# Up weights in six pieces of 512 columns, pair 1's x between the first two, and a new order of work up to pair 4's scores

## The chip, the cores and the metric

One core of one Trainium2 chip runs the whole program. The metric is device time in microseconds (us) of one execution. The engines are TensorE (PE; its weight loads are listed apart as PEld), VectorE (DVE), ScalarE (ACT), GpSimd (POOL) and the sync engine (SP), which only issues transfers. Every engine works through its own list of instructions in order and waits where an operand is not there yet.

## The reference

A chunked state-space recurrence over 4 batches, 8 heads and 768 tokens (x 32 wide, B and C 16 wide) gives y. The 256 values of a token over its heads are the input row of a bilinear feed-forward layer of 1536 hidden columns:

```
L = exp(cum_i - cum_j), causal;  M = (C B^T) * L
y = M x + (C state) * exp(cum);  state = decay * state + B^T (x * decay_from_j)
X = y, as (3072 tokens, 256)
out = ((X @ w_a) * (X @ w_b)) @ w_out        # w_a, w_b: 256 x 1536, w_out: 1536 x 256
```

## The kernel before, in words

The sequence is cut into 6 blocks of 128 tokens. A block has two pairs of batches; pair p is block p // 2, batches 2(p % 2) and the next one. There are 12 pairs. The first four pairs (two blocks, P0 = 4) are done one way, with each of their steps at a place written out by hand; the rest go by loops over blocks.

A pair goes through these steps. Its B, C and x are loaded (`load1`, L140; tiles bn, cn, xn). B and C are scaled by decay factors into bm and cm (`scale_bc`, L291, on POOL or DVE), x into f16 (`scale_x`, L282). PE transposes bm and cm (L326, needs both), ACT and DVE copy them out to bt and ct. `scores` (L353, matmuls at L373 or L358) multiplies them into four PSUM banks; each bank is masked causally into tile t by DVE, or, for the fourth one, by ACT (a copy, L410) and POOL (L411). `pv` (L467) multiplies masked scores with the scaled x (L433), adds the carried state (L477), forms the block's own state sums (`ds_mm`, L460) and evacuates the result into X2T. `state_sums` (L557) and `state_spread` (L569) turn the sums into the next block's carried state, tile sbd, on DVE and POOL.

The feed-forward part of pairs 0 to 3 is cut into units (p, k2), k2 from 0 to 5: a unit is 256 hidden columns, four matmuls of 256 columns against Wa into a bank "aps" and four against Wb into a bank "bps" (`unit_mm`, L596, matmuls at L601). ACT copies aps to SBUF (L615), DVE multiplies with bps into hk (`times`, L622). `out_mm` (L632, matmuls at L637) multiplies hk with Wo, 12 matmuls for each half pair. From block 2 on units have 512 columns (L667) and the output is at L694.

The weights are f32 in memory and are cast to f16 by the transfers that POOL issues. Before, w_a and w_b are loaded in two halves of 768 columns each (`load_w`, L162), w_out in two halves (`load_wo`, L169). A column index k of 128 hidden columns is not contiguous in the piece: it takes every third column of a run of 384 (L601 to L604), so that w_out's rows come as runs of three.

POOL issues these transfers from its own list, between its arithmetic: pair 1's B and C, Wa's first half, Wb's first half, pair 1's x (L211 to L216); after pair 1's B is scaled, Wa's and Wb's second halves and pair 2's B (L768 to L770); after pair 1's masked scores, pair 2's C, w_out's halves and pair 2's x (L797 to L804). SP issues pair 3's inputs and all that follow, in order; pair 3's B waits, by a hand-written dependence (L837), for Wb's last piece to land.

"Warm-up" matmuls on zeros (L220) fill PE's time before there is work. The order of all this is written by hand (`manual_schedule`), and the string BANKS says which of four PSUM banks each successive feed-forward tile takes.

Of the kernel before, what the change touches and what calls it, by code (L numbers as in the profile page):

```python
# [11 lines left out]
f16 = mybir.dt.float16  # L12
# [7 lines left out]
YS = 16.0  # L20

BANKS = (
    "0123102310231012301230123012031230123013201320130213021302130213021320312031203102132013"
    "2013203102310231023103210321032103210321032103210231023102310231023102310231023102310231"
)


# [1 line left out]
def kernel(  # L29
# [13 lines left out]
    nc = tc.nc  # L43
# [39 lines left out]
    big = ctx.enter_context(tc.tile_pool(name="big", bufs=1))  # L83
    a_sb = big.tile([BH, NBLK, Q], f32, name="a_sb")
    zero = big.tile([BH, Q], f32, name="zero")
    KC = d_ff // 2
    Wa = [big.tile([128, 2, KC], f16, name=f"Wa{t}") for t in range(2)]
    Wb = [big.tile([128, 2, KC], f16, name=f"Wb{t}") for t in range(2)]
    Wo = big.tile([128, NK, d_model], f16, name="Wo")
    X2T = big.tile([128, P0, 2, 2, Q], f16, name="X2T")  # L90
    XB = big.tile([128, NBLK - P0 // NBP, 2, 2, NBP, Q], f16, name="XB")
# [35 lines left out]
    def bank(name):  # L127
        return psf.tile([128, 512], f32, name=name, tag=f"ff{next(banks)}")
# [11 lines left out]
    def load1(eng, p, which, bt, i0=0, n=64):  # L140
        blk, bp = divmod(p, NBP)
        if p >= P0:
            return eng.dma_start(
                by_token(pair_in[p][which])[:, bt],
                (B, C, x)[which][2 * bp + bt, :, blk * Q : (blk + 1) * Q, :].rearrange("h q n -> q h n"),
            )
        src = (B, C, x)[which][2 * bp + bt, :, blk * Q + 2 * i0 : blk * Q + 2 * i0 + 2 * n, :]
        return eng.dma_start(  # L148
            pair_in[p][which][64 * bt + i0 : 64 * bt + i0 + n].rearrange("i h r n -> i h (r n)"),
            src.rearrange("h (i r) n -> i h (r n)", r=2),  # L150
        )
# [10 lines left out]
    def load_w(half):  # L162
        c = slice(half * KC, (half + 1) * KC)
        return [
            nc.gpsimd.dma_start(W[half], src.rearrange("(f p) e -> p f e", p=128)[:, :, c])
            for W, src in ((Wa, moe_w_a), (Wb, moe_w_b))
        ]

    def load_wo(half):  # L169
        nc.gpsimd.dma_start(  # L170
            Wo[:, 6 * half : 6 * half + 6].rearrange("p (g kk) e -> p g (kk e)", kk=3),
            moe_w_out.rearrange("(g p kk) e -> p g (kk e)", p=128, kk=3)[:, 2 * half : 2 * half + 2],
        )

    nc.sync.dma_start(a_sb, a.rearrange("b h (k q) -> (b h) k q", q=Q))
    for p_ in range(3):
# [218 lines left out]
    def product0(m2, e):  # L395

        return (
            st[0]["T1"][:, 4 * m2 : 4 * m2 + 4].rearrange("p (m e) r q -> p e m (r q)", e=2)[:, e],
            (SC0, SC1)[m2][:, :, e * 256 : e * 256 + 256],
        )  # L400

    def mask(out_in, by_pool=False, by_token=False):
        o_, i_ = out_in
        if by_token:
            c_ = causal_q.unsqueeze(1).broadcast_to((128, 4, Q))
        else:
            c_ = causal.rearrange("p r q -> p (r q)").unsqueeze(1).broadcast_to((128, 2, 2 * Q))
        if by_pool:
            tmp = mid.tile([128, *c_.shape[1:]], f32, name="tmp", tag="tmp")
            nc.scalar.copy(tmp, i_)  # L410
            nc.gpsimd.tensor_tensor(out=o_, in0=tmp, in1=c_, op=ALU.mult)  # L411
        else:
            nc.vector.tensor_tensor(out=o_, in0=i_, in1=c_, op=ALU.mult)  # L413
# [179 lines left out]
            )  # L593
        st.setdefault(("S", p + NBP), {})["Sbd"] = Sbd

    def unit_mm(p, k2, W):  # L596
        ps = bank("aps" if W is Wa else "bps")
        for kk in range(2):
            k = 2 * k2 + kk
            for f in range(2):  # L600
                nc.tensor.matmul(  # L601
                    ps[:, kk * 2 * Q : (kk + 1) * 2 * Q],
                    W[k // 6][:, f, k % 6 // 3 * 384 : (k % 6 // 3 + 1) * 384].rearrange("p (c kk) -> p kk c", kk=3)[
                        :, k % 3  # L604
                    ],
                    X2T[:, p, :, f],
                    start=(f == 0),
                    stop=(f == 1),
                    skip_group_check=True,
                )  # L610
        return ps

    def evac_a(a_ps, on_dve=False):
        asb = ffh.tile([128, 512], f32, name="asb", tag="asb")
# [44 lines left out]
    def bunit(blk, k):  # L659
        s = st.setdefault(("FF", blk), {})  # L660
        if "hk" not in s:
            s["hk"] = hkb.tile([128, NK, 2 * NBP * Q], f16, name="hkb", tag="hkb")
        ps = []
        for W in (Wa, Wb):
            t_ = bank("aps" if W is Wa else "bps")
            for f in range(2):
                nc.tensor.matmul(  # L667
                    t_,
                    W[k // 6][:, f, k % 6 // 3 * 384 : (k % 6 // 3 + 1) * 384].rearrange("p (c kk) -> p kk c", kk=3)[
                        :, k % 3  # L670
                    ],
                    XB[:, blk - P0 // NBP, f].rearrange("p t j q -> p (t j q)"),
                    start=(f == 0),
                    stop=(f == 1),
                    skip_group_check=True,
                )
# [46 lines left out]
    def go(*items):  # L723
        for p, k2 in items:
            unit(p, k2)()
# [81 lines left out]
    ds_mm(0, 64, SC[:2])  # L807
# [12 lines left out]
    for k2 in range(1, 3):  # L820
        times(0, k2, bps[k2], asb[k2])
# [10 lines left out]
    nc.gpsimd.memset(causal_q, 1.0)  # L832
    nc.gpsimd.affine_select(
        out=causal_q, in_=causal_q, compare_op=ALU.is_ge, fill=0.0, base=0, pattern=[[1, Q]], channel_multiplier=-1
    )
    b3 = [load1(nc.sync, 3, 0, bt) for bt in range(2)]
    tc.add_manual_dep(b3[0].ins, w1[1].ins.name, AFTER, reason="weights ahead of pair 3's inputs")  # L837
    for bt in range(2):
        load1(nc.sync, 3, 1, bt)
    loads_x(3, nc.sync)  # L840
    loads_bc(4)
# [14 lines left out]
    scale_x(2, nc.scalar)  # L856
    scale_bc(3, 0, nc.gpsimd)
    scale_bc(3, 1, nc.gpsimd)
    loads_bc(5)
# [5 lines left out]
    out_mm(0, 1, o[1], range(6, NK))  # L865
    out_store(0, 1, o[1])
    o_ps = bank("ops")
    out_mm(1, 0, o_ps, range(6))
# [187 lines left out]
```

## Time and profile before

| | |
|---|---|
| median of 3 runs | 122.99 us (122.73 to 124.71) |
| the profiled execution | 122.51 us, of which 120.8 us are the span of the profile |
| DVE busy | 85.2 us (71%) |
| ACT busy | 72.1 us (60%) |
| POOL busy | 62.3 us (52%) |
| HBM read and written | 11.13 MB and 3.15 MB |
| busy share of the 16 DMA engines | 0.9 or more in 3 to 24 us, by slices of 3 us |
| SP's wait for Wb's last piece before pair 3's inputs | 13.2 us, until 18.41 us |

Times in the profile are counted from the start of the span. A timeline row gives the start and the length of a run of equal instructions; for PE the length includes the time until the last result is out, so rows overlap and the distance between two starts is the rate. In brackets stands how long the engine was idle before and what ended that. A transfer's row is the time that POOL or SP spent issuing it; how long it took to land is a separate answer.

### The profile page before, as it was taken

The numbers are of one execution on the slowest core, as the hardware profiler recorded it, in microseconds if no ns is written. First come the engines' busy times: TensorE is split into PE (matmuls) and PEld (weight loads), VectorE is DVE, ScalarE is ACT, GpSimd is POOL, SyncE is SP. The second block draws the span as 40 slices with busy tenths as digits, with TensorE's granted clock in tenths as the row PEclk, the third lists the DMA queues.
The fourth block names the chain that finished last, engine by engine and source line by source line (L and its number), as shares of the span: only waits on it lengthen the run. The fifth ranks groups of instructions, "written<-read, shape, count | busy, mean of one in ns | idle before, by whom it ended". The sixth has DMA issues, their size and how long they took to land.

```text
span 120.8 us, 3711 instructions
## 1 busy us (share of the span) xinstructions
PE 115.7 (96%) x1455; PEld 79.4 (66%) x1455; DVE 85.2 (71%) x162; ACT 72.1 (60%) x142; POOL 62.3 (52%) x108
## 2 busy tenths in 40 slices
PE   5889999999999999999999999999999999999990
PEld 2445889888898898644476464766464684555890
DVE  1887888882989898499984999677799445847100
ACT  0466757854965767877668637645646737566220
POOL 7999998972795676299731993138400000000200
PEclk9999999999999999999999999999999999999999
DMA  3999999986969999699998874869501012010032
GB/s 62 171 169 233 173 201 159 215 140 70 100 99 126 128 125 144 111 135 146 71 151 111 173 239 126 91 90 159 180 3 49 0 43 87 0 49 0 20 110 87
DMA packets 66641, 13.73 MB, mean 114 GB/s; under 512 B 61616, under 2 KB 66256, under 8 KB 66624
## 3 DMA queue, kind: packets, MB, share of 16 engines
q1 hardware_dynamic: 62448, 9.40, 50.7%
q0 software_dynamic: 2176, 3.74, 17.0%
q10 hardware_dynamic: 2000, 0.36, 1.6%
q8 instruction: 11, 0.18, 0.7%
q14 instruction: 6, 0.05, 0.1%
HBM read 11.13 MB, written 3.15 MB: 118 GB/s over the span
## 4 chain that ended last, share of the span: by engine, by line
PE 89%; DMA 4%; POOL 3%; issue 0%; ACT 0%; POOLq 0%
PE ops L694 18%; PE aps L667 18%; PE bps L667 17%; PE ops L637 9%; PE aps L601 9%; PE bps L601 9%; DMA Wa<-in_moe_w_a_dram 4%; PE SC L358 2%; PE SC L419 2%; POOL cn L148 1%; PE SC L373 1%; PE SC L433 1%; PE SC L508 1%; POOL bn L148 1%; POOL causal L208 1%; PE SC L460 1%
## 5 line engine op out<-in xcount | busy, mean ns | idle before, releaser
L615 ACT COPY asb<-aps 128x512 f32<-128x512 f32 x72 | 41.8, 586 | 14.1 <-PE aps L667 9.7
L679 DVE TENSOR_TENSOR hkb<-bps,asb 128x512 f16<-128x512 f32 x48 | 32.3, 687 | 12.8 <-ACT asb L615 11.6
L667 PE MATMUL aps<-XB,Wa 128*128 128x512 f16 x96 | 28.6, 379 | 0.0
L667 PE MATMUL bps<-XB,Wb 128*128 128x512 f16 x96 | 28.5, 379 | 0.0
L694 PE MATMUL ops<-Wo,hkb 128*128 128x256 f16 (+1 forms) x204 | 22.5, 267 | 0.0
L694 PEld LDWEIGHTS <-hkb 128*128 128x128 f16 x204 | 18.5, 98 | 3.1
L413 DVE TENSOR_TENSOR t<-SC,causal_q 128x512 f16<-128x512 f32 x27 | 17.1, 681 | 3.3 <-PE SC L358 3.3
L622 DVE TENSOR_TENSOR hk<-bps,asb 128x512 f16<-128x512 f32 x24 | 16.2, 685 | 2.4 <-ACT asb L615 1.2
L667 PEld LDWEIGHTS <-Wb 128*128 128x128 f16 x96 | 9.9, 103 | 10.9
L667 PEld LDWEIGHTS <-Wa 128*128 128x128 f16 x96 | 9.7, 103 | 9.1 <-issue 0.2
L708 POOL DMA_DIRECT2D out_dram<-osb x1 | 0.6, 639 | 27.3 <-ACT osb L706 27.3
L706 ACT ACTIVATE osb<-ops 128x256 f32<-128x256 f32 (+1 forms) x16 | 6.0, 376 | 14.3 <-PE ops L694 14.2
L601 PE MATMUL aps<-X2T,Wa 128*128 128x256 f16 x96 | 14.0, 273 | 0.1
L601 PE MATMUL bps<-X2T,Wb 128*128 128x256 f16 x96 | 13.8, 273 | 0.0
L637 PE MATMUL ops<-Wo,hk 128*128 128x256 f16 x96 | 11.5, 273 | 0.0
L601 PEld LDWEIGHTS <-Wa 128*128 128x128 f16 x96 | 9.5, 104 | 1.1 <-DMA Wa<-in_moe_w_a_dram 0.3
L601 PEld LDWEIGHTS <-Wb 128*128 128x128 f16 x96 | 9.8, 103 | 0.6
L411 POOL TENSOR_TENSOR t<-tmp,causal_q 128x512 f16<-128x512 f32 x5 | 5.8, 1159 | 8.0 <-ACT tmp L410 7.9
L637 PEld LDWEIGHTS <-hk 128*128 128x128 f16 x96 | 8.9, 98 | 1.4
L304 POOL TENSOR_TENSOR bm<-bn,fB 128x256 f16<-128x256 f32 x11 | 7.1, 641 | 4.8 <-DMA bn<-in_B_dram 3.6
L289 POOL TENSOR_SCALAR x<-xn 128x512 f16<-128x512 f32 x6 | 8.9, 1489 | 1.0 <-DMA xn<-in_x_dram 0.7
L296 POOL TENSOR_TENSOR planes<-cn,fC 128x256 f16<-128x256 f32 x8 | 5.0, 621 | 7.9 <-DMA cn<-in_C_dram 7.8
(95 smaller groups left out, 124.0 us busy)
## 6 DMA issues: line engine op xcount, KB each, us to landing
out_dram<-osb SPq DMA_DIRECT2D x22, 128.0 KB, 1.8
xn<-in_x_dram SPq DMA_DIRECT2D x7, 256.0 KB, 4.3
cn<-in_C_dram SPq DMA_DIRECT2D x8, 128.0 KB, 4.1
bn<-in_B_dram SPq DMA_DIRECT2D x8, 128.0 KB, 4.6
Wa<-in_moe_w_a_dram POOLq DMA_DIRECT2D x2, 384.0 KB, 5.9
Wb<-in_moe_w_b_dram POOLq DMA_DIRECT2D x2, 384.0 KB, 7.3
Wo<-in_moe_w_out_dram POOLq DMA_DIRECT2D x2, 384.0 KB, 7.2
xn<-in_x_dram POOLq DMA_DIRECT2D x4, 128.0 KB, 7.2
```

Source lines behind the costliest of these rows:

```text
L289: eng.tensor_scalar(xo, xi, XS, None, ALU.mult)
L304: eng.tensor_tensor(out=m_, in0=raw, in1=(f[:, blk, :, bp] if factor is None else factor).unsqueeze(3).broadcast_to((128, 2, H, N)), op=AL ...
L411: nc.gpsimd.tensor_tensor(out=o_, in0=tmp, in1=c_, op=ALU.mult)
L413: nc.vector.tensor_tensor(out=o_, in0=i_, in1=c_, op=ALU.mult)
L601: nc.tensor.matmul(ps[:, kk * 2 * Q : (kk + 1) * 2 * Q], W[k // 6][:, f, k % 6 // 3 * 384 : (k % 6 // 3 + 1) * 384].rearrange("p (c kk) -> ...
L615: (nc.vector.tensor_copy if on_dve else nc.scalar.copy)(asb, a_ps)
L622: nc.vector.tensor_tensor(out=s["hk"][:, 2 * k2 : 2 * k2 + 2, :].rearrange("p k q -> p (k q)"), in0=b_ps, in1=asb, op=ALU.mult)
L637: nc.tensor.matmul(o_ps[:, 0:d_model], hk[:, k, bt * Q : (bt + 1) * Q], Wo[:, k, :], start=(k == 0), stop=(k == NK - 1), skip_group_check= ...
L667: nc.tensor.matmul(t_, W[k // 6][:, f, k % 6 // 3 * 384 : (k % 6 // 3 + 1) * 384].rearrange("p (c kk) -> p kk c", kk=3)[:, k % 3], XB[:, b ...
L679: return lambda: nc.vector.tensor_tensor(out=s["hk"][:, k], in0=ps[1], in1=asb, op=ALU.mult)
L694: nc.tensor.matmul(o_ps[:, 0:w], hk[:, k, c * Q : (c + 1) * Q], Wo[:, k, cs], start=(k == 0), stop=(k == NK - 1), skip_group_check=True,)
L706: nc.scalar.activation(out=o_sb[:, 0:w], in_=o_ps[:, 0:w], func=AF.Copy, scale=1.0 / (YS * YS))
```

## The change

Wa and Wb become three tiles each of 512 columns, so six pieces. Index k takes every fourth column of a piece (`w_cols`), and w_out's rows come as runs of four, loaded as two thirds and one third. POOL's list becomes: Wa piece 0, pair 1's x, Wb piece 0; then Wa and Wb piece 1; after pair 1's masked scores Wa and Wb piece 2, pair 2's B and C, w_out's two loads; after pair 2's B and C are scaled, pair 2's x and the tile maskbd. The clearing of `planes` and `causal_q` moves behind pair 3's scaling. SP's pair 3 waits for Wb piece 2. On PE two units (0, 0) and (0, 1) instead of three stand ahead of pair 1's `pv`, the second of them split around pair 1's scores; the order of the later units of pairs 0 to 3 changes, one warm-up matmul of 128 columns goes, and the units (2, 4) and (3, 0) come earlier. On DVE the last two scans move ahead. BANKS is another string. From pair 4's scores on the order is as before, but for the unit (3, 0), which has been done.

```diff
-    KC = d_ff // 2
-    Wa = [big.tile([128, 2, KC], f16, name=f"Wa{t}") for t in range(2)]
-    Wb = [big.tile([128, 2, KC], f16, name=f"Wb{t}") for t in range(2)]
+    KG = 4
+    KC = KG * 128
+    Wa = [big.tile([128, 2, KC], f16, name=f"Wa{t}") for t in range(NK // KG)]
+    Wb = [big.tile([128, 2, KC], f16, name=f"Wb{t}") for t in range(NK // KG)]
...
+    def load_w(W, g, f0=0, f1=2):
+        src = (moe_w_a if W is Wa else moe_w_b).rearrange("(f p) e -> p f e", p=128)
+        return nc.gpsimd.dma_start(W[g][:, f0:f1], src[:, f0:f1, g * KC : (g + 1) * KC])
...
+    def w_cols(W, k, f):
+        return W[k // KG][:, f].rearrange("p (c kk) -> p kk c", kk=KG)[:, k % KG]
...
-    load_w(0)
+    load_w(Wa, 0)
     for bt in range(2):
         load1(nc.gpsimd, 1, 2, bt)
+    load_w(Wb, 0)
...
     scores(0)
+    scan(4, 5)
...
     pv_u(0, 1, py, True)
+    scan(5, NBLK)
     for bt in range(2):
         evac0(1, bt, (nc.scalar, nc.vector)[bt], py)
-    scan(4, 5)
-    w1 = load_w(1)
-    for bt in range(2):
-        load1(nc.gpsimd, 2, 0, bt)
-    warmup(1, tcp, 128)
+    load_w(Wa, 1)
+    load_w(Wb, 1)
     transposes(1, apart=True)
-    scan(5, NBLK)
...
-    aps = [unit_mm(0, 0, Wa), unit_mm(0, 1, Wa)]
-    asb = [evac_a(aps[0])]
...
+    aps = [unit_mm(0, 0, Wa)]
+    u1 = unit_mm(0, 1, Wa, (0,))
     scores(1)
     mask(product(1, 3), by_pool=True)
-    aps.append(unit_mm(0, 2, Wa))
-    asb.append(evac_a(aps[1]))
-    asb.append(evac_a(aps[2]))
+    aps.append(unit_mm(0, 1, Wa, (1,), u1))
+    asb = [evac_a(aps[0])]
+    scale_x(1, nc.scalar)
     fps = bank("fps")
     factors(1, NBLK, fps)
-    scale_x(1, nc.scalar)
+    asb.append(evac_a(aps[1]))
     for m in range(3):
         mask(product(1, m))
-    bps = [unit_mm(0, k2, Wb) for k2 in range(3)]
-    for bt in range(2):
-        load1(nc.gpsimd, 2, 1, bt)
-    load_wo(0)
-    nc.gpsimd.tensor_copy(maskbd, headm.unsqueeze(2).broadcast_to((128, H, D)))
-    load_wo(1)
+    bps = [unit_mm(0, k2, Wb) for k2 in range(2)]
+    load_w(Wa, 2)
+    w1 = load_w(Wb, 2)
+    for w in range(2):
+        for bt in range(2):
+            load1(nc.gpsimd, 2, w, bt)
+    load_wo(0, 2)
+    load_wo(2, 3)
     tiles(3)
-    for bt in range(2):
-        load1(nc.gpsimd, 2, 2, bt)
     times(0, 0, bps[0], asb[0])
     pv(1, DS=(0, SC[:2]), split=True)
...
     fb(1)
     scale_bc(2, 0, nc.gpsimd)
     scale_bc(2, 1, nc.gpsimd)
-    go((1, 0), (1, 1), (1, 2))
+    for bt in range(2):
+        load1(nc.gpsimd, 2, 2, bt)
+    nc.gpsimd.tensor_copy(maskbd, headm.unsqueeze(2).broadcast_to((128, H, D)))
+    us = [(0, 2), (0, 3)]
+    asb = [evac_a(unit_mm(p, k2, Wa)) for p, k2 in us]
+    go((1, 0), (1, 1))
+    for (p, k2), a_ in zip(us, asb):
+        times(p, k2, unit_mm(p, k2, Wb), a_)
+    go((1, 2))
+    b3 = [load1(nc.sync, 3, 0, bt) for bt in range(2)]
...
+    go((1, 3))
     state_sums(0)
     state_sums(1)
     state_spread(0)
     state_spread(1)
...
-    for t_ in planes:
-        nc.gpsimd.memset(t_[:, 0:4].bitcast(u32), 0)
...
-    us = [(0, 3), (0, 4), (1, 3)]
-    asb = [evac_a(unit_mm(p, k2, Wa)) for p, k2 in us]
-    for (p, k2), a_ in zip(us, asb):
-        times(p, k2, unit_mm(p, k2, Wb), a_)
-    go((0, 5))
+    go((0, 4), (0, 5))
     transposes(2, apart=True)
...
-    out_mm(0, 0, o[0], range(6))
-    out_mm(0, 1, o[1], range(6))
-    out_mm(0, 0, o[0], range(6, NK))
+    out_mm(0, 0, o[0], range(8))
+    out_mm(0, 1, o[1], range(8))
+    out_mm(0, 0, o[0], range(8, NK))
...
     out_half(1, 1)
-    go((2, 2), (2, 3))
+    go((2, 2), (2, 3), (2, 4))
     pull(3)
     pv(3)
...
-    go((2, 4), (2, 5))
+    go((2, 5), (3, 0))
     scores(4)
...
-    go((3, 0), (3, 1), (3, 2))
+    go((3, 1), (3, 2))
```

More of the change, by code (lines that the diff above doesn't have):

```diff
@@ L22 @@
 BANKS = (
-    "0123102310231012301230123012031230123013201320130213021302130213021320312031203102132013"
-    "2013203102310231023103210321032103210321032103210231023102310231023102310231023102310231"
+    "0123102310321302130213201320312013201321032103210312031203120312031230213021302103123012"
+    "3012302103210321032102310231023102310231023102310321032103210321032103210321032103210321"
 )
@@ L160, in load2, with load_wo @@
         )
[L162 to L169, printed above, removed]
+    def load_w(W, g, f0=0, f1=2):
+        src = (moe_w_a if W is Wa else moe_w_b).rearrange("(f p) e -> p f e", p=128)
+        return nc.gpsimd.dma_start(W[g][:, f0:f1], src[:, f0:f1, g * KC : (g + 1) * KC])
+    def load_wo(g0, g1):
         nc.gpsimd.dma_start(
-            Wo[:, 6 * half : 6 * half + 6].rearrange("p (g kk) e -> p g (kk e)", kk=3),
-            moe_w_out.rearrange("(g p kk) e -> p g (kk e)", p=128, kk=3)[:, 2 * half : 2 * half + 2],
-        )
+            Wo[:, KG * g0 : KG * g1].rearrange("p (g kk) e -> p g (kk e)", kk=KG),
+            moe_w_out.rearrange("(g p kk) e -> p g (kk e)", p=128, kk=KG)[:, g0:g1],
+        )
+    def w_cols(W, k, f):
+        return W[k // KG][:, f].rearrange("p (c kk) -> p kk c", kk=KG)[:, k % KG]
     nc.sync.dma_start(a_sb, a.rearrange("b h (k q) -> (b h) k q", q=Q))
@@ L594, in state_spread, with unit_mm @@
         st.setdefault(("S", p + NBP), {})["Sbd"] = Sbd
[L596 to L599, printed above, removed]
+    def unit_mm(p, k2, W, kks=(0, 1), ps=None):
+        if ps is None:
+            ps = bank("aps" if W is Wa else "bps")
+        for kk in kks:
             for f in range(2):
@@ L602, in unit_mm @@
                     ps[:, kk * 2 * Q : (kk + 1) * 2 * Q],
-                    W[k // 6][:, f, k % 6 // 3 * 384 : (k % 6 // 3 + 1) * 384].rearrange("p (c kk) -> p kk c", kk=3)[
-                        :, k % 3
-                    ],
+                    w_cols(W, 2 * k2 + kk, f),
                     X2T[:, p, :, f],
@@ L668, in bunit @@
                     t_,
-                    W[k // 6][:, f, k % 6 // 3 * 384 : (k % 6 // 3 + 1) * 384].rearrange("p (c kk) -> p kk c", kk=3)[
-                        :, k % 3
-                    ],
+                    w_cols(W, k, f),
                     XB[:, blk - P0 // NBP, f].rearrange("p t j q -> p (t j q)"),
@@ L819 @@
     nc.scalar.copy(G.rearrange("p b g -> p (b g)"), gps[:, 0 : nb * NG])
-    for k2 in range(1, 3):
-        times(0, k2, bps[k2], asb[k2])
+    times(0, 1, bps[1], asb[1])
     fb(1)
@@ L824 @@
     scale_bc(2, 1, nc.gpsimd)
-    go((1, 0), (1, 1), (1, 2))
+    for bt in range(2):
[8 more added lines that the diff above has]
+    b3 = [load1(nc.sync, 3, 0, bt) for bt in range(2)]
+    tc.add_manual_dep(b3[0].ins, w1.ins.name, AFTER, reason="weights ahead of later inputs")
+    for bt in range(2):
+        load1(nc.sync, 3, 1, bt)
+    loads_x(3, nc.sync)
+    loads_bc(4)
+    go((1, 3))
     state_sums(0)
@@ L829 @@
     state_spread(1)
-    for t_ in planes:
-        nc.gpsimd.memset(t_[:, 0:4].bitcast(u32), 0)
[L832 to L841, printed above, removed]
-    us = [(0, 3), (0, 4), (1, 3)]
-    asb = [evac_a(unit_mm(p, k2, Wa)) for p, k2 in us]
-    for (p, k2), a_ in zip(us, asb):
-        times(p, k2, unit_mm(p, k2, Wb), a_)
-    go((0, 5))
+    go((0, 4), (0, 5))
     transposes(2, apart=True)
@@ L858 @@
     scale_bc(3, 1, nc.gpsimd)
+    for t_ in planes:
+        nc.gpsimd.memset(t_[:, 0:4].bitcast(u32), 0)
+    nc.gpsimd.memset(causal_q, 1.0)
+    nc.gpsimd.affine_select(
+        out=causal_q, in_=causal_q, compare_op=ALU.is_ge, fill=0.0, base=0, pattern=[[1, Q]], channel_multiplier=-1
+    )
     loads_bc(5)
     o = [bank("ops"), bank("ops")]
-    out_mm(0, 0, o[0], range(6))
-    out_mm(0, 1, o[1], range(6))
-    out_mm(0, 0, o[0], range(6, NK))
+    out_mm(0, 0, o[0], range(8))
+    out_mm(0, 1, o[1], range(8))
+    out_mm(0, 0, o[0], range(8, NK))
     out_store(0, 0, o[0])
-    out_mm(0, 1, o[1], range(6, NK))
+    out_mm(0, 1, o[1], range(8, NK))
     out_store(0, 1, o[1])
```

## The prediction

> **What bounds the kernel now.** I read the page's busy shares and slices first, to see which engine sets the time and from when.
>
> ```profile
> PE 115.7 (96%) x1455; PEld 79.4 (66%) x1455; DVE 85.2 (71%) x162; ACT 72.1 (60%) x142; POOL 62.3 (52%) x108
> ...
> PE   5889999999999999999999999999999999999990
> ...
> PEclk9999999999999999999999999999999999999999
> ```
>
> PE is busy 96% of the span at the full granted clock, and from the fourth slice (9 us) nearly without a gap. Only the first three slices and the end are open. The chain of waits, cut to the first 22 us, says what releases PE there:
>
> ```profile
> 3.75 1.35 POOL cn L148 x2
> 5.11 5.43 DMA Wa<-in_moe_w_a_dram
> 10.54 0.05 issue
> 10.58 1.06 PE aps L601 x8
> 11.64 0.36 PE SC L373 x32
> 12.00 0.55 PE aps L601 x4
> ```
>
> POOL issues Wa's first half at 5.11; it lands at 10.54 and the first unit starts. After that the chain is PE alone to the last output. So the sum needs two things: how much earlier PE can start in earnest, and whether anything in the new order makes PE wait afterwards. PE's timeline at that place:
>
> ```profile
> 9.73 0.23 PE L220 MATMUL tc<-warm 128*128 128x128 f16 x1
> 10.05 0.29 PE L326 MATMUL SC<-ident,bm 128*128 128x128 f16 x2
> 10.17 0.28 PE L326 MATMUL SC<-ident,cm 128*128 128x128 f16 x2
> 10.58 1.06 PE L601 MATMUL aps<-X2T,Wa 128*128 128x256 f16 x8
> 11.57 0.43 PE L373 MATMUL SC<-ct,bt 32*64 32x128 f16 x32
> ```
>
> The transposes at 10.05 wait for bm from POOL (9.17 + 0.82 = 9.99). Everything ahead of that is filler or pair 0's own chain, which the change doesn't touch. So PE gains at most 10.58 less about 10.29 (transposes from 10.05, 0.12 for two).
>
> POOL's timeline is the other one, because its list also issues the transfers:
>
> ```profile
> 8.05 1.16 POOL L411 TENSOR_TENSOR t<-tmp,causal 128x512 f16<-128x512 f32 x1
> 9.17 0.82 POOL L304 TENSOR_TENSOR bm<-bn,fB 128x256 f16<-128x256 f32 x1
> 9.94 0.74 POOL L165 DMA_DIRECT2D Wa<-in_moe_w_a_dram  x1
> 10.67 0.73 POOL L165 DMA_DIRECT2D Wb<-in_moe_w_b_dram  x1
> 11.37 1.43 POOL L148 DMA_DIRECT2D bn<-in_B_dram  x2
> ...
> 13.55 1.16 POOL L411 TENSOR_TENSOR t<-tmp,causal 128x512 f16<-128x512 f32 x1
> ```
>
> **The head, worked out.** The issues of Wa, Wb and x's two pieces (5.11, 5.83, 6.55, 7.27) took 5.4, 7.0, 6.8 and 6.7 to land, so landings near 10.54, 12.83, 13.3 and 14.0. One 384 KB piece takes 12.83 - 10.54 = 2.3 us of the queue, so a third of it is 0.75. Wa's piece 0 lands at 10.54 - 0.75 = 9.8, before the transposes: PE starts at 10.29, 0.29 earlier. Then six matmuls (4 take 0.44 in the chain; 0.65, and 0.1 to change shape) to 11.05; the scores wait for bt (ACT 10.48 + 0.84 = 11.32) and end near 11.6, where before they ended at 11.93. So PE is 0.35 ahead: this is the whole gain. The lost warm-up matmul (0.12) gives nothing, as PE waited for bm behind it.
>
> The rest of the head must be covered. The second half of unit (0, 1) and the factors (12.48 to 13.31 before) bring PE to 12.75, where Wb's piece 0 is needed. It now stands behind x: by bytes it lands at 14.0 - 2 x 0.75 = 12.5, covered by 0.25. Two Wb units (0.87) bring PE to 13.65. There `pv` of pair 1 needs DVE's three masks (0.63 each from 11.7: 13.6), POOL's (13.4) and the scaled x (x lands at 14.0 less a third of Wa and all of Wb, about 11; scaled at 13.4). With 1.04 for pv, sums and G (14.73 to 15.77 before) PE is at 14.7. One unit fewer is done than before, so 0.87 of work has only moved behind.
>
> **Later weight pieces.** Wa's piece 1 is issued at 9.94 as before. The second half landed at 9.94 + 6.3 = 16.2 (Wb's at 10.67 + 7.7 = 18.4), so by bytes it lands at 16.2 - 3 x 0.75 = 13.95; if the queue had run dry it needs at most Wa's 5.4 less 0.75, so 14.6: covered at 14.7. Wb's piece 1 (15.4 to 16.0) is needed at 17.3. Piece 2 is queued on POOL behind hr, hs, hsx and the mask (ready for it at 12.2, 1.16 long), so at 13.4 and 14.1; with 4.7 to 5.4 us to landing it is there at 18.1 to 19.5. PE needs it at 14.7 + 0.87 (two Wa units) + 1.74 + 0.87 + 1.74 = 19.9. Covered by 0.4 to 1.8; uncovered, each late microsecond is one of PE. The two more issues cost POOL 2 x 0.74 = 1.5 us, and these fall ahead of pair 2's inputs.
>
> **What comes late next: pair 2.** Its B was issued at 11.37, its C at 14.65. Now B goes at 14.85 and C at 16.3 and 16.95. Before:
>
> ```profile
> cn<-in_C_dram POOLq DMA_DIRECT2D x1, 64.0 KB, 4.8
> ```
>
> is the second piece of C. With 4.3 (pair 1's C, emptier queue) to 4.8 it lands at 21.25 to 21.75, so cm (0.62) is done at 21.9 to 22.4. PE reaches the transposes of pair 2 (L326) at 19.9 + 1.74 = 21.65, before at 21.91. I take 22.05 for the second two transposes: a stall of 0.3, and the lead of 0.35 is down to about 0. DVE's state sums, which must leave the same banks, end near 21.7 by a count of its list (0.69 per product, 0.85 for the sums): equal rank, no more. Queued on PE behind a late cm are the last two units of pair 1, scores and all of pair 2.
>
> w_out: the queue carries the same bytes, but has two short gaps at 10.2 and 13.5 (no piece issued yet), together 0.8 by the distance between the last byte of one and the next issue. So 24.1 and 25.4 against 22.7 and 24.8 before; PE needs them at 24.3 and 26.1 (16 matmuls by 0.113). Nearly no cover for the first: 0 to 0.2.
>
> Pair 2's x: two issues, now behind bm and cm on POOL, at 22.05 and 22.8 (before 17.81 and 18.55). SP's pieces of the same size took 5.2 and 5.9 in that window, ACT's 4.0 on an emptier one, and this load itself 7.6 behind two w_out pieces issued up to 1.8 us ahead. Now w_out is 3.6 us ahead, so I take 4.5, between SP's and ACT's: 27.3, scaled (0.63) at 27.95; pv of pair 2 would be reached at about 27.9 (27.93 before). Stall 0 to 1.1, taken at 0.1. POOL's own list (maskbd 0.4, two sbd and gU 3.1, mask 1.16 from 23.5) ends at 28.1, when the last heads need it. bm and cm of pair 3 then end at 29.4, 0.2 ahead of their transposes.
>
> **Pairs 3 and 4.** SP starts on Wb's piece 2, about 0.8 later than 18.41, and its later issues shift with it. Pair 4's scores (37.28) had their turned operand at 32.80 + 3.4 = 36.2, 1.1 of cover; with (3, 0) moved ahead of them they come 0.87 later. Covered. The clearing of planes (1.1 us of POOL) falls in POOL's wait for pair 4's C (27.96 to 30.14 before). `pv` of pair 3 needs POOL's mask (ends 34.62 before, needed about 35.1); (2, 4) ahead of it adds 0.87. Covered. (3, 0), (2, 4) are moved, not added: nothing in the sum. The scans, BANKS and w_out's grouping cost nothing: DVE waits 0.45 where the scan lands, and no wait of PE for a bank is in the profile.
>
> **Sum**: -0.35 at the head, +0.3 at pair 2's transposes, +0.1 at its x: 0.05 more than nothing, or 122.55 against the profiled execution's own 122.51 (span 120.8 and 1.7 around it). The median of the three runs is 0.5 above that execution, so 123.0 there.
>
> A rule bears on the weights' new step. A weight load of contiguous hk takes 98 ns, of Wa at a step of 6 bytes 104, and the matmuls follow each other at 0.1092 us (12 in 1.31):
>
> ```profile
> L601 PEld LDWEIGHTS <-Wa 128*128 128x128 f16 x96 | 9.5, 104 | 1.1 <-DMA Wa<-in_moe_w_a_dram 0.3
> ...
> L637 PEld LDWEIGHTS <-hk 128*128 128x128 f16 x96 | 8.9, 98 | 1.4
> ```
>
> If these 6 ns are the price of the wider step, 8 bytes cost about 107, still below 109: nothing in the sum. The Trainium skill (SBUF — State Buffer, "Door 1: The DMA port swizzle") says that reads keep full bandwidth with at least two hits in each 16-byte line and pay beyond it; steps of 6 and 8 bytes make 2.7 and 2 hits, so by that rule the new step is just free. The trace agrees for 6 bytes within its 6 ns; none here shows 8.
>
> **Rivals.** *The cover holds*: C and x of pair 2 land as fast as on an emptier queue (4.0 to 4.3) and most of the 0.35 stays. For it: the queue's gap at 13.5 leaves less ahead of them than before; against it: POOL's C is 1.6 us later by its own list. Time 122.99 - 0.35 = 122.6. Chance 0.25.
>
> *Pair 2's x is late* (slower): if its last piece takes its old 7.6 us, it lands at 22.8 + 7.6 = 30.4, is scaled at 31.0, and PE waits 3.1 at pv of pair 2 in place of the 0.1: 126.0. Against it: w_out is further ahead. From 7.0 us to landing on it decides for slower by over 2%; from 5 to 7 it gives 123.5 to 125.4. Chance 0.12, a third of it beyond 2%.
>
> *The weights' step costs*: loads above 109 ns set the pace of the 192 matmuls at L601; at 125 ns (as if the 6 ns per step grew fourfold) that is 192 x 0.016 = 3 us, so 126. The 512-column units (217 ns a matmul) hide it. Against: 103 for 6 bytes. Chance 0.05.
>
> *The change doesn't do what it says*: Wa's piece 0 takes its 5.4 whatever its size, the start stays at 10.58, and the stalls of pair 2 remain partly: 123.2. Chance 0.08.
>
> **How the numbers follow.** The forecast has 0.50: 123.0, its own range 122.5 to 123.6 (stalls of 0 to 1). The range 122.2 to 124.7 takes in the rival with the full gain and the runs' own scatter below (0.3), and x's lateness up to 6.3 us to landing. Faster by over 2% (about what a measurement of this kernel can tell from no change; below 120.5) would need 2.5 us from a head that offers 0.35: 0.02. Slower by over 2% (above 125.5): 0.04 from x, 0.04 from the step, 0.02 for several misses in a row: 0.10. Within: 0.88.
>
> **What would show it.** Right: the first L601 at about 10.3 with no wait for Wa, pair 1's scores done at 11.6; PE's transposes of pair 2's C waiting for cm at about 22; the first 128x512 unit at 50.0, as before, give or take 0.3. Wrong: PE waiting for Wb at 12.7 or for piece 2 at 19.9; weight loads of Wa above 109 ns; a wait at pv of pair 2 over 1 us.

## The result, and the profile after

The changed kernel takes 125.04 us (median of 6 runs, 124.65 to 125.71) against 123.26 us for the kernel before on the same chip (6 runs, 122.61 to 124.71). The ratio is 1.015 with a 95% interval of 1.011 to 1.019: slower by 1.8 us, and the time lies above the range forecast. Medians are taken over all runs, ratios and intervals over those outside the chip's slower state, in which a run takes longer. Its profiled execution took 124.9 us with a span of 123.2, where the one before had 122.51 and 120.8. Line numbers of the changed kernel differ by a few from those of before (L603 is the old L601, L328 the old L326, L375 the old L373; L435 are the `pv` matmuls, the old L433).

The busy shares and the slices of the profile after:

```profile
PE 116.1 (94%) x1454; PEld 82.5 (67%) x1454; DVE 85.5 (69%) x162; ACT 72.1 (59%) x142; POOL 63.8 (52%) x110
...
PE   5888999996999999899999999999999999999990
```

PE's work is the same (116.1 us against 115.7), at the same full granted clock; its share fell because the span grew. The 6 in the tenth slice (27.7 to 30.8 us) is new. From the chain of waits, the parts that matter here:

```profile
12.63 1.17 POOL t L413
13.80 0.70 POOL Wa L165
14.50 6.36 DMA Wb<-in_moe_w_b_dram
...
23.36 5.63 DMA xn<-in_x_dram
...
29.07 0.64 ACT x L289
```

Before, the chain left the transfers at 10.54 and was PE's alone from there. Now it goes through two more: Wb's last piece, 6.4 us on its way and issued behind GpSimd's mask of pair 1 and Wa's piece 2, and the second piece of pair 2's x, 5.6. PE's timeline gives the waits themselves:

```profile
10.09 0.29 PE L328 MATMUL SC<-ident,bm 128*128 128x128 f16 x2 [0.26 <-POOL bm L306]
...
10.32 0.96 PE L603 MATMUL aps<-X2T,Wa 128*128 128x256 f16 x6
11.41 0.43 PE L375 MATMUL SC<-ct,bt 32*64 32x128 f16 x32
...
12.95 1.06 PE L603 MATMUL bps<-X2T,Wb 128*128 128x256 f16 x8
13.94 0.42 PE L435 MATMUL SC<-t,x 64*32 64x128 f16 x32
...
20.90 0.63 PE L603 MATMUL bps<-X2T,Wb 128*128 128x256 f16 x4 [0.22 <-DMA Wb<-in_moe_w_b_dram]
...
22.73 0.28 PE L328 MATMUL SC<-ident,cm 128*128 128x128 f16 x2 [0.21 <-POOL cm L306]
...
29.76 0.42 PE L435 MATMUL SC<-t,x 64*32 64x128 f16 x32 [1.03 <-ACT x L289]
...
52.00 0.40 PE L360 MATMUL SC<-turned 32*128 32x128 f16 x16 [0.42 <-ACT osb L650]
```

In the kernel before, the same places at pair 2 have no bracket:

```profile
21.91 0.28 PE L326 MATMUL SC<-ident,bm 128*128 128x128 f16 x2
22.02 0.28 PE L326 MATMUL SC<-ident,cm 128*128 128x128 f16 x2
...
23.97 0.43 PE L373 MATMUL SC<-ct,bt 32*64 32x128 f16 x32
...
27.93 0.42 PE L433 MATMUL SC<-t,x 64*32 64x128 f16 x32
```

The brackets after name five waits. The first, 0.26 for bm, stands where a warm-up matmul stood before. The others are new: 0.22 for Wb's piece 2, 0.21 for pair 2's C (with 0.2 lost beside each: four matmuls start 0.82 after the four before them, where 0.44 is the usual distance, and the second pair of transposes 0.49 after the first, where 0.11 is the usual one), 1.03 for pair 2's x and 0.42 at pair 6's scores. Against the kernel before, the same places of PE's list start as follows (us):

| place | before | after | late |
|---|---|---|---|
| first unit | 10.58 | 10.32 | -0.26 |
| pair 1's scores (two matmuls, 0.22, fewer done) | 11.57 | 11.41 | +0.06 with these counted |
| `pv` of pair 1 (one unit, 0.87, fewer done) | 14.73 | 13.94 | +0.08 with the unit counted |
| pair 2's scores (same work done) | 23.97 | 24.69 | +0.72 |
| `pv` of pair 2 (same work done) | 27.93 | 29.76 | +1.83 |
| pair 5's scores | 41.65 | 43.49 | +1.84 |
| pair 6's scores | 49.67 | 52.00 | +2.33 |
| first 512-column unit | 50.01 | 52.33 | +2.32 |

So the loss is 0.72 by pair 2's scores, 1.11 more by its `pv`, 0.49 more by pair 6's scores. GpSimd's timeline shows what moved the transfers:

```profile
9.98 0.76 POOL L165 DMA_DIRECT2D Wa<-in_moe_w_a_dram  x1
...
13.74 0.76 POOL L165 DMA_DIRECT2D Wa<-in_moe_w_a_dram  x1
...
15.21 1.42 POOL L149 DMA_DIRECT2D bn<-in_B_dram  x2
...
21.46 0.62 POOL L306 TENSOR_TENSOR bm<-bn,fB 128x256 f16<-128x256 f32 x1 [2.17 <-DMA bn<-in_B_dram]
22.06 0.61 POOL L306 TENSOR_TENSOR cm<-cn,fC 128x256 f16<-128x256 f32 x1
22.62 1.45 POOL L149 DMA_DIRECT2D xn<-in_x_dram  x2
```

From w_out's issues (17.95 to 19.29) GpSimd stands idle for 2.17 until pair 2's B has landed, then scales B and C, and only then issues x, which before it had issued at 17.81, ahead of the scaling. And between Wb's piece 1 (10.72 to 11.44) and Wa's piece 2 (13.74) it issued nothing, since hr, hs, hsx and the mask stand there. The window from 14.75 to 16.0 us in the table of transfer queues shows the trace of that on GpSimd's queue (its packets, MB, share of 16 engines):

```profile
q0 software_dynamic: 85, 0.08, 67.1%
```

In the same window of the kernel before:

```profile
q0 software_dynamic: 176, 0.26, 117.2%
```

There are three such stretches after: 11 to 12.25 (0.08 MB against 0.34), 14.75 to 16 (0.08 against 0.26) and 19.75 to 20.75 (0.08 against 0.16).

### The profile page after: what moved, and what is told of

It is laid out like the page before. It is cut to its first block, busy times and chain, and to the rows that moved or that the text cites. A ratio compares the mean times of both kernels' runs of the same rounds, so it can differ in the third digit from the quotient of the medians.

```text
span 123.2 us, 3710 instructions
## 1 busy us (share of the span) xinstructions
PE 116.1 (94%) x1454; PEld 82.5 (67%) x1454; DVE 85.5 (69%) x162; ACT 72.1 (59%) x142; POOL 63.8 (52%) x110
## 4 chain that ended last, share of the span: by engine, by line
PE 75%; DMA 10%; POOL 8%; ACT 2%; issue 1%; DVE 1%; ACTq 0%; POOLq 0%
PE ops L693 18%; PE aps L668 17%; PE bps L668 17%; PE ops L638 6%; DMA Wb<-in_moe_w_b_dram 5%; PE bps L603 5%; PE aps L603 5%; DMA xn<-in_x_dram 5%; PE SC L360 2%; PE SC L421 2%; POOL t L413 1%; POOL Wa L165 1%; POOL xn L149 1%; POOL cn L149 1%; PE SC L510 1%
## 5 line engine op out<-in xcount | busy, mean ns | idle before, releaser
L668 PEld LDWEIGHTS <-Wb 128*128 128x128 f16 x96 | 10.9, 114 | 9.9
L668 PEld LDWEIGHTS <-Wa 128*128 128x128 f16 x96 | 10.6, 114 | 8.2 <-issue 0.2
L603 PE MATMUL aps<-X2T,Wa 128*128 128x256 f16 x96 | 14.3, 274 | 0.0
L603 PE MATMUL bps<-X2T,Wb 128*128 128x256 f16 x96 | 14.0, 273 | 0.2 <-DMA Wb<-in_moe_w_b_dram 0.2
L603 PEld LDWEIGHTS <-Wb 128*128 128x128 f16 x96 | 10.4, 114 | 0.5 <-DMA Wb<-in_moe_w_b_dram 0.5
L603 PEld LDWEIGHTS <-Wa 128*128 128x128 f16 x96 | 10.2, 114 | 0.4 <-DVE X2T L552 0.2
(95 smaller groups left out, 125.4 us busy)
```

What stands on the lines that cost most here:

```text
L603: nc.tensor.matmul(ps[:, kk * 2 * Q : (kk + 1) * 2 * Q], w_cols(W, 2 * k2 + kk, f), X2T[:, p, :, f], start=(f == 0), stop=(f == 1), skip_g ...
L668: nc.tensor.matmul(t_, w_cols(W, k, f), XB[:, blk - P0 // NBP, f].rearrange("p t j q -> p (t j q)"), start=(f == 0), stop=(f == 1), skip_g ...
```

## The experiments

The profiles suggest two causes in a row: the queue runs low at 14.75 because Wa's piece 2 is issued too late, which costs the waits for Wb and C; and pair 2's x is issued too late, which costs the wait at `pv`. The rivals were the weights' step of four columns, x between the first weight pieces, the split unit, SP's later start (its release moved from 18.41 to 20.92), and the two units moved ahead. Medians and intervals are against runs of the kernel before on the same chip, 122.86 to 123.05 us in the four groups.

**Pair 2's x earlier on GpSimd's list.** In the changed kernel:

```diff
     load_wo(0, 2)
     load_wo(2, 3)
+    for bt in range(2):
+        load1(nc.gpsimd, 2, 2, bt)
...
     scale_bc(2, 1, nc.gpsimd)
-    for bt in range(2):
-        load1(nc.gpsimd, 2, 2, bt)
```

> The changed kernel with pair 2's x issued right behind w_out, ahead of bm and cm of pair 2 on GpSimd. Theory place (x is late because its issue stands behind bm and cm): its second piece is issued at about 20.9 instead of 23.36 (it waits for Wb's piece 2, whose semaphore it shares), lands by 26.5 instead of 28.99, TensorE's wait of 1.1 us at pair 2's pv is gone, and the time falls by 1.1 to 1.6 us: ratio to the kernel before about 1.005. Rival queue (x comes when the queue has moved the bytes ahead of it): it lands only where w_out lets it, 27 to 28, the wait falls by 0.5 or less, ratio 1.010 or more. Rival step (weights at every fourth column): no change, 1.015.

Measured: 124.01 us, ratio 1.008 (1.005 to 1.011). GpSimd's timeline:

```profile
19.93 0.71 POOL L149 DMA_DIRECT2D xn<-in_x_dram  x1 [0.66 <-DMA Wa<-in_moe_w_a_dram]
21.13 0.69 POOL L149 DMA_DIRECT2D xn<-in_x_dram  x1 [0.48 <-DMA Wb<-in_moe_w_b_dram]
```

The issues waited 0.66 and 0.48 for the landing of pieces issued eight transfers earlier, so x left at 19.93 and 21.13 and not at 19.3 and 20.0; it took 6.4 and 6.1 us to land. Even so, `pv` of pair 2 follows at 29.03 without a wait for x, while 0.23 for Wb and 0.29 for C remain. The scaling of pair 2's B now stands behind x's two waiting issues (21.84, in the changed kernel 21.46), and pair 2's scores start at 25.07 instead of 24.69, so this order gains less than the wait that it removes. The lateness of x is one cause, worth 0.7% here, and not the whole.

**Wa's piece 2 ahead of GpSimd's arithmetic.**

```diff
     load_w(Wa, 1)
     load_w(Wb, 1)
+    load_w(Wa, 2)
     transposes(1, apart=True)
...
-    load_w(Wa, 2)
     w1 = load_w(Wb, 2)
```

> The changed kernel with Wa's piece 2 issued at about 11.5, right behind Wb's piece 1 and ahead of hr, hs, hsx and pair 1's mask on GpSimd, instead of at 13.74. Theory gaps (the queue runs dry between the pieces, because the next one is issued behind GpSimd's arithmetic and its first bytes come some 2.3 us after the issue): the low stretch of the queue at 14.75 to 16.25 fills, Wb's piece 2 and pair 2's B land about 1.2 us sooner (19.7 and 20.2), cm by 21.5, x by 28, and the time falls by 0.8 to 1.3 us, less 0.2 for the mask that comes 0.35 later: ratio 1.005 to 1.01. Rival place: pieces sooner but x hardly, below 0.4 us gained. Rival step: 1.015.

Measured: 124.05 us, ratio 1.008 (1.005 to 1.011). Wa's piece 2 is issued at 11.46, Wb's at 14.05. GpSimd's queue in 14.75 to 16.0 us:

```profile
q0 software_dynamic: 212, 0.20, 103.3%
```

The low stretch is filled. PE's timeline:

```profile
22.13 0.27 PE L328 MATMUL SC<-ident,cm 128*128 128x128 f16 x2
...
28.78 0.42 PE L435 MATMUL SC<-t,x 64*32 64x128 f16 x32 [0.67 <-ACT x L289]
```

The waits for Wb and for C are gone (no bracket at 22.13, and pair 2's scores at 24.08 against 24.69); the wait for x remains, 0.67. The other stretch, at 11 to 12.25, is still there (0.07 MB) and costs nothing here: no unit waits for Wa's or Wb's piece 1.

**Both together.** The two diffs above in one kernel.

> The changed kernel with both: Wa's piece 2 ahead of hr, and pair 2's x issued right behind w_out. Theories gaps and place as two causes in a row: TensorE reaches pair 2's scores at 24.1 as with the first edit alone and pair 2's pv at 28.1 with no wait for x; the first 512-column unit starts at 50.2, ratio 1.000 to 1.003. Rival one cause (each edit removes the same wait): pv at 28.8 as with one edit alone, ratio 1.006 to 1.008.

Measured: 123.14 us (12 runs), ratio 1.0014 (0.9994 to 1.0034), no difference that can be told. PE's timeline:

```profile
22.06 0.27 PE L328 MATMUL SC<-ident,cm 128*128 128x128 f16 x2
...
27.98 0.42 PE L435 MATMUL SC<-t,x 64*32 64x128 f16 x32
```

Neither has a wait, and `pv` of pair 2 is 0.05 from its place before (27.93). Each edit alone gives back 0.7 of the 1.5%, the two together all of it: two causes, each with its own share, and everything else in the change together is worth nothing that these runs can tell. (Ratios of different groups of runs can differ by 0.5% for one kernel, as the repeat further down shows; but the kernel with the step of two columns, whose order is that of the changed kernel, ran in the same group as the two single edits and stood at 1.015.) In this profile pair 5's scores come 0.2 late and pair 6's wait 0.41, so that wait is not theirs.

**The kernel before with x late.** In the kernel before, the same x loop moved from behind `tiles(3)` to behind the scaling of C:

```diff
     tiles(3)
-    for bt in range(2):
-        load1(nc.gpsimd, 2, 2, bt)
...
     scale_bc(2, 1, nc.gpsimd)
+    for bt in range(2):
+        load1(nc.gpsimd, 2, 2, bt)
```

> The kernel before with only pair 2's x moved behind bm and cm of pair 2 on GpSimd, so issued at about 20 and 20.9 instead of 17.81 and 18.55. Theory place alone: x lands 2.2 us later (28.4), TensorE waits about 1 us at pair 2's pv, ratio 1.008. Theory gaps (the place matters only with bm and cm late): x lands by 26.5, about as before, no wait, ratio 1.000.

Measured: 123.46 us, ratio 1.004 (1.0001 to 1.008), between the two. The interval only just leaves out 1, so this run doesn't tell what the place alone costs. In its profile `pv` of pair 2 starts 4.16 after pair 2's scores, where the kernel before has 3.96, so 0.2 is lost there; another 0.3 is lost by those scores, by a gap at 15.6 us for which the profile names nothing. And pair 2's C took 5.3 to 6.2 us to land where the kernel before, with the same list up to there, took 4.5 to 4.8, so x went out at 22.19, later than in the expectation.

**The weights' step of two columns.** Index k takes every second column of a quarter of the piece, w_out's rows in runs of two:

```diff
-        return W[k // KG][:, f].rearrange("p (c kk) -> p kk c", kk=KG)[:, k % KG]
+        c0 = k % KG // 2 * 256
+        return W[k // KG][:, f, c0 : c0 + 256].rearrange("p (c kk) -> p kk c", kk=2)[:, k % 2]
```

> The changed kernel with every second column instead of every fourth as the step of a weight load, and w_out's rows in runs of two; all transfers and the order as they are. Rival step: weight loads fall from 114 ns to about 101, TensorE gains, ratio 1.005 or less. Theories place and gaps: weight loads shorter all the same, but matmuls at the same distance (0.4375 us for four), ratio 1.015 as it is.

Measured: 124.89 us, ratio 1.015 (1.011 to 1.019), as without the edit. Its weight loads take 98 ns on average, the changed kernel's 114, and the distance between matmuls is the same. Its PE waited at other places (1.09 for w_out, whose rows come in shorter runs here and whose first load took 7.8 us to land, in the changed kernel 6.2, and 0.57 for x), so the equal time is not a clean one; the distance of the matmuls is.

**The step made worse in the kernel before.** Step 6 columns, w_out in runs of six:

```diff
-    W[k // 6][:, f, k % 6 // 3 * 384 : (k % 6 // 3 + 1) * 384].rearrange("p (c kk) -> p kk c", kk=3)[:, k % 3]
+    W[k // 6][:, f].rearrange("p (c kk) -> p kk c", kk=6)[:, k % 6]
```

> The kernel before with every sixth column as the step of a weight load (12 bytes) instead of every third, and w_out's rows in runs of six. If the load's price goes on growing as from 98 ns (step of 4 bytes) to 104 (6) and 114 (8), it is about 130 ns, longer than the 109 ns of a 256-column matmul: four matmuls at L601 take 0.52 us instead of 0.437, 192 of them 4 us more in all, ratio 1.03; the 512-column ones stay at 217 ns. If the load overlaps regardless, ratio 1.00.

Measured: 123.15 us, ratio 1.003 (1.0006 to 1.0056). The group of its weight loads (busy us and mean ns behind the bar), and of the changed kernel's:

```profile
L601 PEld LDWEIGHTS <-Wa 128*128 128x128 f16 x96 | 10.4, 126 | 0.3
```

```profile
L603 PEld LDWEIGHTS <-Wa 128*128 128x128 f16 x96 | 10.2, 114 | 0.4 <-DVE X2T L552 0.2
```

PE's timeline of the kernel with step 6:

```profile
16.68 0.60 PE L601 MATMUL aps<-X2T,Wa 128*128 128x256 f16 x4
17.12 0.60 PE L601 MATMUL bps<-X2T,Wb 128*128 128x256 f16 x4
```

A load of 126 ns is longer than the 109 ns from one matmul to the next, and still four matmuls start 0.44 after the four before them, as with loads of 104 ns. The step has no share in the time, and the 0.3% of this run is at most what the rest of the edit (w_out's runs, and spread) is worth.

**SP released earlier.** SP's loads of pair 3 wait for Wb's piece 1 instead of piece 2:

```diff
-    load_w(Wb, 1)
+    w1 = load_w(Wb, 1)
...
-    w1 = load_w(Wb, 2)
+    load_w(Wb, 2)
```

> The changed kernel with the sync engine's loads of pair 3 and later released by Wb's piece 1 instead of piece 2, so from about 16 instead of 20.9. Theory gate (the 0.48 us that TensorE loses at pair 6's scores come from the sync engine's late start): these scores lose nothing more against pair 5's (8.0 us between the two instead of 8.5), the waits of pair 2 stay or grow by up to 0.5 as more transfers share the engines; ratio 1.011 to 1.019. Rival: the loss at pair 6 stays, as it follows TensorE's own lateness.

Measured: 126.3 us, ratio 1.024 (1.019 to 1.029): worse than the changed kernel. SP starts at 15.77 instead of 20.92. PE's timeline:

```profile
24.45 0.28 PE L328 MATMUL SC<-ident,cm 128*128 128x128 f16 x2 [1.50 <-POOL cm L306]
...
32.06 0.42 PE L435 MATMUL SC<-t,x 64*32 64x128 f16 x32 [1.61 <-ACT x L289]
```

Pair 2's C, issued at the same 16.6, took 6.3 to 6.4 us to land instead of 4.5 to 5.0, and w_out 7.8 and 8.8 instead of 6.2 and 7.3; everything behind C on GpSimd's list went late. These landings are of one profile each, but the ratios (1.024 and 1.015) point the same way: SP's late start protects GpSimd's transfers, and it costs nothing at pair 3. The wait at pair 6 is missing here, as in several others, so that is no mark of SP's start.

**Pair 2's B and C ahead of the last weight pieces.**

```diff
-    load_w(Wa, 2)
-    w1 = load_w(Wb, 2)
     for w in range(2):
         for bt in range(2):
             load1(nc.gpsimd, 2, w, bt)
+    load_w(Wa, 2)
+    w1 = load_w(Wb, 2)
```

> The changed kernel with pair 2's B and C issued ahead of Wa's and Wb's piece 2. Theory gaps: B and C land by 19.5, TensorE's wait for cm is gone, but the pieces come about 0.7 us later behind the same empty queue, so the units (0, 4) wait for Wa or Wb by 0.7 to 1 us; x is issued about 1.5 us earlier and its wait shrinks: ratio 1.008 to 1.012. Rival order alone (B's and C's place behind the two pieces is the whole cause): all waits gone, ratio 1.000 to 1.003.

Measured: 125.93 us, ratio 1.022 (1.017 to 1.027), worse than either expectation. Besides 0.21 for Wa's piece 0, which the edit doesn't touch, PE waits 0.30 for Wa's piece 2 at 20.66, 0.61 for Wb's at 21.90 and 0.56 for w_out at 26.28, then 0.77 for GpSimd's mask and 0.61 for the turned operand of pair 6. C is in time. In this order the four issues of 64 KB (2.8 us of GpSimd) stand before 512 KB that PE needs first.

**x between the first weight pieces.** Pair 1's x behind Wb's piece 0:

```diff
     load_w(Wa, 0)
+    load_w(Wb, 0)
     for bt in range(2):
         load1(nc.gpsimd, 1, 2, bt)
-    load_w(Wb, 0)
```

> The changed kernel with pair 1's x behind Wb's piece 0, as before the change. If pair 1's x between the pieces matters to the loss or to the head: Wb's piece 0 lands some 0.7 us sooner and x some 0.8 us later (12.1), which its scaling at 12.93 still covers, and the first Wb unit does not move from 12.95, since the factors end there; ratio 1.015, no effect. If x there is what made the queue run dry at 11 us, Wa's piece 1 lands differently by 0.3 or more and the ratio moves by 0.003.

Measured: 124.24 us, ratio 1.009 (1.006 to 1.013), which looked like a third cause, though the two found already filled the 1.5%. So it was repeated beside the changed kernel itself, in one group:

> The changed kernel with pair 1's x behind Wb's piece 0, a second time. Theory that x between the first pieces is a part of the loss: 1.008 to 1.011, below the unaltered kernel by 0.004 or more. Rival, spread: within 0.003 of it.

> The changed kernel itself, unaltered, beside the next two. If the edit of x_after_wb0 matters, this one stays at 1.013 to 1.016 and that one at 1.008 to 1.011; if its 1.0094 was the spread of landing times from execution to execution, the two come within 0.003 of each other.

Measured: 124.69 us, ratio 1.014 (1.012 to 1.017), and 124.73, ratio 1.015 (1.012 to 1.018). The two are equal, and the first value was spread between groups, of 0.5%: an interval made of one group's runs doesn't hold that spread. In the repeated profile of the changed kernel the wait for x is 1.28 and pair 6's scores don't wait at all.

**All three orders together.**

> The changed kernel with all three: Wa's piece 2 ahead of hr, pair 2's x right behind w_out, pair 1's x behind Wb's piece 0. If the x between is a part of the loss of its own: 0.996 to 0.999, faster than the two edits alone (1.0014). If not: 1.000 to 1.003.

Measured: 123.13 us (12 runs), ratio 1.0025 (0.999 to 1.006). From the transposes at 10.13 us to the first 512-column unit (50.14, before 50.01) no wait is marked in its PE timeline; it is no faster than the kernel before. So with all of PE's new waits gone the change's own gain is nil, and the 0.26 at the first unit brings nothing.

**The split unit undone.** Both cures, and unit (0, 1) whole before pair 1's scores:

```diff
-    u1 = unit_mm(0, 1, Wa, (0,))
+    aps.append(unit_mm(0, 1, Wa))
     scores(1)
...
-    aps.append(unit_mm(0, 1, Wa, (1,), u1))
```

> The same, and the unit (0, 1) no longer split around pair 1's scores: its four Wa matmuls stand ahead of them. Theory bt (TensorE waits some 0.3 us for bt of pair 1 there, so the head's earlier start is lost to the split): pair 1's scores still start at 11.4, the first Wb unit comes 0.2 us sooner (12.73 instead of 12.95), and if no wait takes it back the first 512-column unit starts at 50.0, ratio 0.998 to 1.002. Rival (the split is worth having): scores later by 0.2, nothing gained.

Measured: 123.31 us, ratio 1.003 (1.001 to 1.004). The Wb units come earlier (12.68 against 12.95), and then `pv` of pair 1 waits 0.23 for DVE's masks and starts at 14.09. The place of the unit gives nothing either way.

**(3, 0) back behind pair 4's scores.** Both cures, and

```diff
-    go((2, 5), (3, 0))
+    go((2, 5))
     scores(4)
...
-    go((3, 1), (3, 2))
+    go((3, 0), (3, 1), (3, 2))
```

> The changed kernel with Wa's piece 2 ahead of hr, pair 2's x right behind w_out, and the unit (3, 0) back behind pair 4's scores. Theory cover (moving (3, 0) puts pair 4's scores, and with them GpSimd's list up to pair 6's operand, 0.87 us later against TensorE, which then waits 0.2 at pair 5's and 0.4 at pair 6's scores): pair 4's scores start at 37.3 with no wait, 8.0 us between pair 5's and pair 6's scores, first 512-column unit at 50.1, ratio 0.995 to 0.999. Rival late operand (pair 4's operand, 0.8 us later than before through the sync engine's later start, needs that cover): TensorE waits at pair 4's scores, 37.3 becomes 37.6 or more, and the first 512-column unit stays at 50.5 or later, ratio 1.001 to 1.003.

Measured: 123.55 us, ratio 1.006 (1.004 to 1.008). Pair 4's scores wait here: the first two matmuls start at 37.59, the other fourteen at 37.98, after DVE's U. So in this order (3, 0) is cover, as the kernel has it, and moving it ahead has not cost the 1.5%. PE also waits 0.20 at 15.04 for Wa's piece 1 in this profile, so the queue's first low stretch is not without cost in every execution.

## Why the prediction was wrong, by its steps

The forecast of 123.0 failed, and so did its range; the rival "pair 2's x is late" is what happened, by a part of its price, with a second wait in front of it.

- **"So PE is 0.35 ahead: this is the whole gain."** The start was right (10.29 said, 10.32 measured), and Wa's smaller piece did land sooner (4.5 us on its way). The rest of the step was not: the scores wait for bt (ready at 11.36) and not for the units, so they start at 11.41, 0.16 sooner than before but with two matmuls (0.22) fewer done: the lead is gone there already. So the factors came at 12.12, the first Wb unit at 12.95 (12.75 said) and `pv` of pair 1 at 13.94 (13.65 said). The step's own rows show it: bt at 11.32 and 0.36 of scores end at 11.7, 0.25 ahead of 11.93, and the two matmuls take 0.22 of that. With the unit that moved behind counted, PE is 0.08 late at `pv` and 0.08 ahead behind it (14.82, before 15.77). The two kernels with both cures (in one of them no wait is marked up to the first 512-column unit) confirm it: the head is worth nothing. I had counted the lead at its start and not at the next operand, pair 1's bt, which comes at the same time in both kernels.
- **"The queue ... has two short gaps ..., together 0.8 by the distance between the last byte of one and the next issue."** This is the step that failed first. The gap lasts until the next piece's bytes come at the full rate, and that is 2.3 to 2.5 us after the issue starts: Wa's piece 1 was issued at 9.98 and the queue was full again at 12.4; piece 2 at 13.74 and full at 16.25. The measured stretches are three, each of 1.0 to 1.25 us at a quarter to a half of the rate. Piece 2 was also issued 0.3 to 0.4 later than said, as GpSimd's mask waited 0.39 for ACT's copy. Hence Wb's piece 2 took 6.4 us to land (4.7 to 5.4 said), pair 2's B 5.4 and 5.9, and the cover "by 0.4 to 1.8" was -0.4 (0.22 of it marked as a wait). The experiment with Wa's piece 2 issued 2.3 earlier fills the second stretch, Wb's piece 2 takes 5.5 there, and the waits for Wb and C are gone. The Trainium skill (DMA: Bandwidth & Descriptors, "Specifications") gives about 1 us to the first byte for transfers issued by GpSimd; no view here tells the first byte apart from the last ones of the piece before. What the forecast needed is the time to the full rate, and for a cast weight piece on a queue that has run low that is the measured 2.3 to 2.5.
- **Pair 2's C, "a stall of 0.3".** The price of C itself was about right (4.5 and 5.0 us to landing, 4.3 to 4.8 said). I had it waiting at 22.05 and it came at 22.73, because B, which I had not priced, held GpSimd until 21.46. The stall there and at Wb made 0.72 in all, in place of 0.3 less the lead.
- **Pair 2's x, "stall 0 to 1.1, taken at 0.1".** Issued at 22.62 and 23.36, 0.57 later than said, and 5.3 and 5.6 us on its way (4.5 taken from between SP's and ACT's rows, although SP's rows, 5.2 and 5.9, were of that very window). The wait was 1.03. The rival gave 123.5 to 125.4 for 5 to 7 us to landing; 125.04 lies in it, but not by the rival's price alone: by its scale 5.6 us gives about 124.1, and the rest is the later issue and the stalls in front. The experiment with x ahead of the scaling takes this wait away and 0.7% with it.
- **The weights' step.** That "loads above 109 ns set the pace" was wrong as a rule, though it changed nothing in the sum. The loads rose to 114 ns, where I had said about 107, and the mark named in the forecast (loads above 109) was met without effect; loads of 126 ns have none either. The rule of the Trainium skill quoted there (SBUF — State Buffer, "Door 1: The DMA port swizzle"), by which two hits in a 16-byte line are free, does not fit the loads: 98 ns contiguous and at 4 bytes, 104 at 6 bytes, 114 at 8, 126 at 12. At 8 bytes a line has its two hits and the load is 16 ns longer all the same.
- **What held.** w_out landed at 24.1 and 25.9 (24.1 and 25.4 said) without a wait. Pairs 3 and 4 were covered, though SP started 2.5 us after 18.41 and not 0.8. No wait is seen at the units moved ahead, and (3, 0) moved back gained nothing.
- **Pair 6's scores.** 0.42 of wait that the forecast hadn't. The bracket names ACT's osb, but that can't be it: in the repeated profile of the same program the scores start (51.87) before that osb does (51.97). They wait for pair 6's turned operand, which a transposing transfer issued by SP brings.

SP's row of that transfer in the changed kernel:

```profile
46.56 2.09 SPq L350 DMA_TRANSPOSE turned<-planes  x1
```

It took 5.4 us to land, so until 51.96, and the scores start at 52.00; with both cures it was issued at 44.80 and took 5.6, and the scores start at 50.41. In the repeated profile it was issued at 46.59 and took 3.5, and nothing waits. Of the 16 profiles, eight have 3.4 to 3.5 us here and eight 5.2 to 5.6, and kernels of the old and the new order are among each. In the old order (the kernel with the step of six) 5.2 us, from 44.41, are just covered: its scores start at 49.71 without a marked wait. Why the transfer takes one or the other time stays open. SP released earlier and (3, 0) moved back, the two edits whose expectations asked about this wait, both had the short time and so don't test it.

The medians differ by 1.78 us, the first 512-column units of the two profiled executions by 2.32: the profiled one of the kernel before lies 0.75 under the median of its six runs, and the wait at pair 6 is not in every execution. So the sum has, in place of -0.35 at the head and 0.3 at pair 2's transposes, 0.72 for head, Wb and C together, and 1.11 in place of 0.1 at x.

## What to carry to other kernels

Cutting a load in pieces makes the queue drain sooner, so each next piece must be issued earlier by the time from its issue to the full rate, here 2.3 to 2.5 us; look at what stands before it on the issuing engine's list, arithmetic above all. A transfer issued behind work that itself waits for a transfer is late by both landings in a row; issue it first, as long as the queue has nothing more urgent. And an earlier start of the bound engine is counted at the next operand that it waits for, not at the start.

## What the runs showed of the hardware

- From the start of an issue on GpSimd to the full rate of its queue, when that had run low: 2.3 to 2.5 us for 256 KB weight pieces, cast on the way.
- An issue on GpSimd can itself wait: x's two issues stood 0.66 and 0.48 us until Wa's and Wb's piece 2, which were issued eight transfers before, had landed.
- With SP's loads issued 5.1 us earlier, GpSimd's 64 KB loads of pair 2's C took 6.3 to 6.4 us instead of 4.5 to 5.0 (one profile each), though the queues are two.
- A weight load longer (126 ns) than the distance of the 256-column matmuls (109 ns) didn't stretch that distance.
- The same transfers on the same list took 4.5 to 4.8 us in one execution and 5.3 to 6.2 in another, and the transposing transfer of one operand 3.4 to 3.5 or 5.2 to 5.6; a cover under 1 us lies within this spread.
